# The first loads of a fused FFT-mix and gated MLP: a quarter on another queue, and two splits in another order

## The chip, the core and the metric

The kernel runs on one core of a Trainium2 chip. Such a core has a matrix engine (TensorE, PE in the profile, with its weight loads shown apart as PEld), VectorE (DVE), ScalarE (ACT), GpSimd (POOL) and SyncE (SP). Each engine works through its own list of instructions in order, and they wait for one another and for DMA transfers through semaphores. SyncE and GpSimd both issue DMA transfers here, each through a queue of its own, and all transfers share 16 DMA engines.

The metric is the device time of one launch in microseconds (us), the median over runs. The kernel before takes 355.21 us, the median of three runs between 354.94 and 356.22.

## The reference

For an input `x` of 2048 rows and 512 columns, the kernel computes a blend of two results, with a gate per row:

```python
x = A_x
g = _sigmoid((x * gate_w).sum(-1, keepdims=True))
# a: real part of a two-dimensional DFT of x
a_re, a_im = x @ dft_hid_re.T, x @ dft_hid_im.T
a = dft_seq_re @ a_re - dft_seq_im @ a_im
# b: gated MLP, 512 -> 1376 -> 512
b = (silu(x @ w1) * (x @ w3)) @ w2
return g * a + (1 - g) * b
```

All operands are float32.

## The kernel before, in words

**Precision.** TensorE multiplies float32 values that were rounded to a shorter form. To keep float32 accuracy, each operand is split into a rounded high part and a remainder. `high` (line 115) writes the high part with a copy on ACT; `low` (line 118) subtracts it from the source on DVE and writes the remainder; `split` does the one and then the other. A product of two operands is then three products on TensorE: high with high, high with remainder, remainder with high (line 129). The contraction of 256 rows takes two steps of 128, so a "chain" in this text is six products of 128x512 into one bank of PSUM.

**Stages.** The first and longest stage computes the two matrices `x @ w1` and `x @ w3` for 11 blocks of 128 columns, two halves of the rows each, with a scheme of seven products per two-by-two block (the factors of x are named B11, B12, B21, B22 and sums T1 to T4). Intermediate rows go out to HBM through GpSimd's queue and come back later. The second stage multiplies them by `w2` (H in the profile), the third does the DFT (O, E and Y), and the last one blends and writes the result.

**The opening.** This is where the change is made. The very first block is computed in another way than the rest, so that TensorE can begin on little data. The array `first` is laid out by the host as 3072 columns for 128 partitions: the first weight quarter (256 columns), B11 (1024), the fourth weight quarter (256), the second weight quarter (256), B21 (1024), the third weight quarter (256). SyncE loads it into `raw` in four loads of 768 columns (line 417). The first of them holds the first weight quarter and the first half of B11, the second one the second half of B11 and the fourth quarter. The third and fourth load do the same for B21. After them SyncE loads B12 and B22 (`xs_B`, line 174) and the next weights (`ws`, line 198).

While the loads are under way, TensorE runs nine products of a constant (line 423, `wps`, the number is `WARM`), whose result is not used, and ACT loads its table.

Then ACT and DVE split what has come, in a written order (the kernel sets the order of all instructions by hand). `high_by_both` has the first 256 columns of a half block rounded by ACT and the other 256 by DVE (line 465, CAST). `split_by_both` does this and then has DVE write the remainder of the whole half. Weights are split into `wa`, the fourth quarter into `a`, and x into `xo`. The chains (`C` in the profile) follow: the first with the first weight quarter and B11, the second with the fourth quarter and B11, the third with the second quarter and B21, the fourth with the third quarter and B21, and then the four chains with B12 and B22. In a chain's first step the first half of the block is used, in the second step the second half; the last of the six products needs the remainder of the second half.

The names and lines to follow: `raw<-first` (line 417) are the first loads, `wps` (423) the constant's products, line 115 ACT's rounding, 118 DVE's remainders, 465 DVE's share of rounding, 129 the products. Behind the edit the lines of the changed kernel are two lower.

Of the kernel before, what the change touches and what calls it, by code (L numbers as in the profile page):

```python
# [18 lines left out]
NTB = S // TB  # L19
NC = (F + P - 1) // P  # L20
NP2 = (NC + 1) // 2
WARM = 9
LOOK = 3
K = 9
TOL = 2.0 ** 40
# [5 lines left out]
def fnet_swiglu_gate_kernel(  # L31
# [27 lines left out]
    nc = tc.nc  # L59
# [26 lines left out]
    def bank(k, name):  # L86
        return psum.tile([P, 512], F32, tag=f"ps{k}", name=name)
# [26 lines left out]
    def high(hi, src):  # L114
        nc.scalar.activation(hi, src, AF.Copy)  # L115

    def low(hi, lo, src):
        nc.vector.tensor_sub(lo, src, hi.bitcast(F32))  # L118

    def split(hi, lo, src):  # L120
        high(hi, src)
        low(hi, lo, src)
# [20 lines left out]
    def flat(ap):  # L143
        return ap.rearrange("p a n -> p (a n)")
# [268 lines left out]
    ctx.enter_context(tc.manual_schedule())  # L413
    XO[0] = xo0.tile([P, 2, 7, 2, 512], F32R, tag="xo", name="xo0")
    raw = xo1.tile([P, 2, 6, 2, 512], F32, tag="xo", name="raw")[:, 0].rearrange("p i q n -> p (i q n)")
    for n in range(4):
        nc.sync.dma_start(raw[:, 768 * n : 768 * n + 768], first[:, 768 * n : 768 * n + 768])
    ST[0, "B11"], ST[0, "B21"] = raw[:, 256:1280], raw[:, 1792:2816]
    W0 = [raw[:, at : at + 256] for at in (0, 1536, 2816, 1280)]
    warm = nc.const_aps.tensor(1.0, [P, 512], mybir.dt.bfloat16)  # L420
    wps = bank(7, "wps")
    for n in range(WARM):
        nc.tensor.matmul(wps, warm[:, :P], warm, start=True, stop=True)
# [11 lines left out]
    def half(i, j, w, x, start):  # L435

        wp = lambda h, sl: a21[:, h, sl] if w is None else WA[0][:, h, w, sl]
        xp = lambda q, h: b12[:, h, q * 512 : (q + 1) * 512] if x is None else XO[0][:, h, x, q, :]  # L440
        hh, lh, hl = (0, 0), (1, 0), (0, 1)
        order = [(r, *p) for r in range(2)
                 for p in ((hh, lh, hl) if x is None or r and w == x else (hh, hl, lh))]
        for n, (r, u, v) in enumerate(order):
            matmul(C[i, j], wp(u, slice(r * P, (r + 1) * P)), xp(r, v),
                   start=start and n == 0, stop=not start and n == 5)

    def xo_half(k, q):
        i = OPS.index(k)
        return XO[0][:, 0, i, q], XO[0][:, 1, i, q], ST[0, k][:, q * 512 : (q + 1) * 512]  # L450
# [12 lines left out]
    def high_by_both(hi, lo, src):  # L463
        high(hi[:, :256], src[:, :256])
        nc.vector.tensor_copy(hi[:, 256:], src[:, 256:])

    def split_by_both(hi, lo, src):
        high_by_both(hi, lo, src)
        low(hi, lo, src)

    def w0_parts(w):
        return flat(WA[0][:, 0, w : w + 1]), flat(WA[0][:, 1, w : w + 1]), W0[w]

    high_by_both(*xo_half("B11", 0))
    high(*w0_parts(0)[::2])
    low(*xo_half("B11", 0))
    low(*w0_parts(0))
    split(*xo_half("B11", 1))
    half(0, 0, 0, 0, True)
    split(a21[:, 0], a21[:, 1], W0[3])  # L480
    half(1, 0, None, 0, True)
# [91 lines left out]
    n = NI - 1 - LOOK  # L573
# [1057 lines left out]
```

## Time and profile before

| | us |
|---|---|
| median of three runs | 355.21 |
| lowest, highest | 354.94, 356.22 |
| the profiled execution | 355.75 |
| its span, first to last instruction | 354.0 |
| PE busy in the span | 348.0 |
| DVE busy | 311.2 |
| ACT busy | 233.5 |
| first instruction on the constant, PE | 0.91 |
| first product of real data, PE | 5.17 |

The profile is of one execution. Times count from the start of the span, and the span is shorter than the device time, since the launch lies around it. A row of the timeline gives start, length, engine, line, operation, tile written and tiles read, shape and number, and in brackets the idle time of the engine ahead of it, with what ended that. A row of the busy time by stretch gives the stretch, its length, and then busy time and count for PE, PEld, DVE, ACT and POOL, the granted TensorE clock, the share of the DMA engines and GB/s. The ends of products are modelled: a product is shown 0.38 us long though in a full stream the next one starts earlier. The rows of DMA issues give the size of one and the time from its issue to its landing.

### The profile page before, as it was taken

The numbers are of one execution on the slowest core, as the hardware profiler recorded it, in microseconds if no ns is written. First come the engines' busy times: TensorE is split into PE (matmuls) and PEld (weight loads), VectorE is DVE, ScalarE is ACT, GpSimd is POOL, SyncE is SP. The second block draws the span as 40 slices with busy tenths as digits, with TensorE's granted clock in tenths as the row PEclk, the third lists the DMA queues.
The fourth block names the chain that finished last, engine by engine and source line by source line (L and its number), as shares of the span: only waits on it lengthen the run. The fifth ranks groups of instructions, "written<-read, shape, count | busy, mean of one in ns | idle before, by whom it ended". The sixth has DMA issues, their size and how long they took to land.

```text
span 354.0 us, 5152 instructions
## 1 busy us (share of the span) xinstructions
PE 348.0 (98%) x1718; PEld 303.7 (86%) x1718; DVE 311.2 (88%) x442; ACT 233.5 (66%) x395; POOL 73.3 (21%) x121
## 2 busy tenths in 40 slices
PE   8999999999999999999999999999999999999994
PEld 4888888888888888888888888888888888889994
DVE  4999989999869788888887899989969989998983
ACT  5875866556648687775433399642588988879940
POOL 0012333323111132111113763335011002000000
PEclk9999999999999999999999999999999999999999
DMA  7669865669645779999999149997649999999276
GB/s 279 254 244 357 319 261 212 224 240 332 222 120 192 250 218 390 408 400 402 373 382 291 58 126 373 410 365 241 237 120 362 416 411 406 411 409 348 100 262 219
DMA packets 33952, 103.03 MB, mean 291 GB/s; under 512 B 5874, under 2 KB 6276, under 8 KB 33924
## 3 DMA queue, kind: packets, MB, share of 16 engines
q1 hardware_dynamic: 26340, 75.91, 58.2%
q0 software_dynamic: 7584, 26.77, 20.6%
q8 instruction: 14, 0.23, 0.3%
q14 instruction: 14, 0.11, 0.1%
HBM read 78.02 MB, written 24.65 MB: 290 GB/s over the span
## 4 chain that ended last, share of the span: by engine, by line
PE 96%; DMA 1%; ACT 1%; DVE 0%; issue 0%; SPq 0%; ACTq 0%
PE H L129 32%; PE X L129 30%; PE Z L129 15%; PE Y L129 8%; PE Y L1304 4%; PE C L129 3%; PE O L129 3%; PE E L129 1%; DMA raw<-first 1%; PE Yodd L1304 0%; DVE h L408 0%; ACT w2t L115 0%; ACT u L369 0%; DVE r L1358 0%; ACT xo L115 0%
## 5 line engine op out<-in xcount | busy, mean ns | idle before, releaser
L129 PE MATMUL H<-w2t,ht 128*128 128x512 f32 (+1 forms) x528 | 114.1, 379 | 0.0
L129 PEld LDWEIGHTS H<-w2t,ht 128*128 128x128 f32 (+1 forms) x528 | 99.8, 189 | 14.2
L129 PE MATMUL X<-xo,wb 128*128 128x512 f32 x378 | 88.6, 379 | 0.0
L129 PEld LDWEIGHTS X<-xo,wb 128*128 128x128 f32 x378 | 71.4, 189 | 10.2
L765 ACT ACTIVATE t<-t 128x1024 f32<-128x1024 f32 (+1 forms) x68 | 67.3, 992 | 1.5 <-DVE t L754 1.4
L320 POOL DMA_DIRECT2D hs<-h x36 | 19.6, 545 | 88.7 <-DVE h L391 63.5
L404 ACT ACTIVATE h<-X 128x512 f32<-128x512 f32 x21 | 12.5, 596 | 32.2 <-PE X L129 21.8
L129 PE MATMUL Z<-xo,wa 128*128 128x512 f32 x126 | 30.7, 380 | 0.0
L129 PE MATMUL X<-xo,wa 128*128 128x512 f32 x126 | 30.8, 380 | 0.0
L115 ACT ACTIVATE ht<-hr 128x1024 fp32r<-128x1024 f32 x19 | 20.0, 1053 | 16.3 <-PE H L129 10.6
L129 PE MATMUL Y<-xo,wa 128*128 128x512 f32 x126 | 30.6, 379 | 0.0
L129 PE MATMUL Z<-xo,wb 128*128 128x512 f32 x126 | 30.6, 379 | 0.0
L381 DVE TENSOR_TENSOR u<-u,X 128x512 f32<-128x512 f32 x21 | 14.4, 686 | 17.9 <-PE X L129 13.4
L129 PEld LDWEIGHTS Z<-xo,wa 128*128 128x128 f32 x126 | 23.7, 189 | 3.8 <-ACT u L369 0.4
L129 PEld LDWEIGHTS X<-xo,wa 128*128 128x128 f32 x126 | 23.7, 189 | 3.6 <-DVE wa L118 0.3
L129 PEld LDWEIGHTS Y<-xo,wa 128*128 128x128 f32 x126 | 23.8, 189 | 3.4
L129 PEld LDWEIGHTS Z<-xo,wb 128*128 128x128 f32 x126 | 23.8, 189 | 3.4
L754 DVE TENSOR_TENSOR t<-t,rep 128x1024 f32<-128x1024 f32 x21 | 24.7, 1220 | 0.6 <-DMA t<-wt 0.6
L118 DVE TENSOR_TENSOR ht<-hr,ht 128x1024 fp32r<-128x1024 f32 x19 | 23.1, 1217 | 0.0
L115 ACT ACTIVATE wa<-ws 128x768 fp32r<-128x768 f32 x19 | 15.9, 838 | 6.2 <-PE Z L129 5.9
L752 DVE TENSOR_TENSOR t<-t,rep 128x512 f32<-128x512 f32 x30 | 19.0, 684 | 0.0
L756 DVE TENSOR_TENSOR t<-t,rep 128x1024 f32<-128x1024 f32 x16 | 18.7, 1220 | 0.0
(210 smaller groups left out, 519.6 us busy)
## 6 DMA issues: line engine op xcount, KB each, us to landing
t<-wt SPq DMA_DIRECT2D x60, 512.0 KB, 9.3
hr<-hs SPq DMA_DIRECT2D x19, 512.0 KB, 8.8
hs<-h POOLq DMA_DIRECT2D x36, 256.0 KB, 4.4
wbsp<-wb POOLq DMA_DIRECT2D x16, 512.0 KB, 4.8
wb<-wbsp SPq DMA_DIRECT2D x16, 512.0 KB, 9.4
xr<-xw SPq DMA_DIRECT2D x8, 512.0 KB, 11.6
xs_B<-xt SPq DMA_DIRECT2D x6, 512.0 KB, 6.5
ws<-w POOLq DMA_DIRECT2D x6, 512.0 KB, 4.0
```

The costliest lines, as they stand in the source:

```text
L115: nc.scalar.activation(hi, src, AF.Copy)
L118: nc.vector.tensor_sub(lo, src, hi.bitcast(F32))
L129: nc.tensor.matmul(ps.rearrange("p (n a) -> p n a", a=2), u, turns(v)[:, some], **kw)
L320: nc.gpsimd.dma_start(hs[c][:, b * TB : (b + 1) * TB], h)
L381: nc.vector.tensor_add(u4, u4, x)
L404: nc.scalar.activation(g1, x, AF.Silu)
L752: f(*(v[:, 512 * a : 512 * a + 512] for v in (t, t, r)))
L754: nc.vector.tensor_sub(t, t, r)
L756: nc.vector.tensor_add(t, t, r)
L765: nc.scalar.activation(t[:, :n], t[:, :n], AF.Abs, accum_out=acc[:, i : i + 1])
L1304: nc.tensor.matmul(to, u[i], v[j], start=n == k == 0, stop=n == len(terms) - 1 and k == 2, skip_group_check=True)
```

## The change

The first 256 columns of `first`, the first weight quarter, are loaded through GpSimd's queue. SyncE's first load holds only the 512 columns of the first half of B11; its three others are as they were. The quarter is split first, on ACT and then on DVE, and only then the first half of B11. The second half of B11 is rounded by ACT and DVE together, where before ACT rounded it alone. The number of products of the constant goes from nine to eight.

```diff
-WARM = 9
+WARM = 8
...
-    for n in range(4):
-        nc.sync.dma_start(raw[:, 768 * n : 768 * n + 768], first[:, 768 * n : 768 * n + 768])
+    for n, (lo, hi) in enumerate(((0, 256), (256, 768), (768, 1536), (1536, 2304), (2304, 3072))):
+        (nc.sync if n else nc.gpsimd).dma_start(raw[:, lo:hi], first[:, lo:hi])
...
-    high_by_both(*xo_half("B11", 0))
-    high(*w0_parts(0)[::2])
-    low(*xo_half("B11", 0))
-    low(*w0_parts(0))
-    split(*xo_half("B11", 1))
+    split(*w0_parts(0))
+    split_by_both(*xo_half("B11", 0))
+    split_by_both(*xo_half("B11", 1))
     half(0, 0, 0, 0, True)
```

The first rows of DVE's list, from the first instruction on data (`wa` is the quarter, `xo` is B11, `a` the fourth quarter; in brackets what an instruction waits for: DMAHW is a load of SyncE by its number, DMASW one of GpSimd, Activation is ACT):

```order
+L118 TENSOR_TENSOR wa_135<-raw,wa_135 128x256 [waits DMASW0_49,Activation_49]
 L465 CAST xo_100<-raw 128x256 [waits DMAHW0_49]
 L118 TENSOR_TENSOR xo_100<-raw,xo_100 128x512 [waits DVE_49,Activation_49]
-L118 TENSOR_TENSOR wa_135<-raw,wa_135 128x256 [waits Activation_49]
-L118 TENSOR_TENSOR xo_100<-raw,xo_100 128x512 [waits DMAHW1_49,Activation_49]
+L465 CAST xo_100<-raw 128x256 [waits DMAHW1_49]
+L118 TENSOR_TENSOR xo_100<-raw,xo_100 128x512 [waits DVE_49,Activation_49]
 L118 TENSOR_TENSOR a_128<-raw,a_128 128x256 [waits Activation_49]
```

The quarter's remainder moved from third place to the first, ahead of everything on x, and a second CAST stands ahead of the second remainder of B11.

The same place in ACT's list:

```order
+L115 ACTIVATE wa_135<-raw 128x256 [waits DMASW0_49]
 L115 ACTIVATE xo_100<-raw 128x256 [waits DMAHW0_49]
-L115 ACTIVATE wa_135<-raw 128x256
-L115 ACTIVATE xo_100<-raw 128x512 [waits DMAHW1_49]
+L115 ACTIVATE xo_100<-raw 128x256 [waits DMAHW1_49]
 L115 ACTIVATE a_128<-raw 128x256
```

The quarter's rounding moved ahead of that of x and waits for GpSimd's load, and the rounding of the second half of B11 has 256 columns where it had 512.

## Prediction

> **What bounds the kernel now.** I read the page first, for the engine that is full and the chain that ended last.
>
> ```profile
> span 354.0 us, 5152 instructions
> PE 348.0 (98%) x1718; PEld 303.7 (86%) x1718; DVE 311.2 (88%) x442; ACT 233.5 (66%) x395; POOL 73.3 (21%) x121
> ...
> PE 96%; DMA 1%; ACT 1%; DVE 0%; issue 0%; SPq 0%; ACTq 0%
> ...
> L129 PE MATMUL H<-w2t,ht 128*128 128x512 f32 (+1 forms) x528 | 114.1, 379 | 0.0
> ```
>
> TensorE is busy for 98% of the span and makes up 96% of the chain. One product of 512 columns costs 114.1 / 528 = 0.216 us in a full stream. The 1% of DMA and the ACT before the first product are where the edit lies, so next I read the chain of waits in order of time, and the busy time by stretch.
>
> ```profile
> 0.84 3.54 DMA raw<-first
> 4.38 0.02 issue
> 4.40 0.42 ACT xo L115
> 4.82 0.32 ACT wa L115
> 5.17 11.21 PE C L129 x48
> ...
> 9.37:207.22 197.85, 197.80 (x916) 172.59 (x915) 174.86 (x276) 123.57 (x207) 50.23 (x96) 1.00 0.76 274
> ```
>
> The first load lands at 4.38, two ACT instructions follow, and the first real product starts at 5.17. Behind 9.37 the TensorE column (the first after the length) is as long as the stretch, to 0.05 us in 198, and the chain stays on TensorE after it. So whatever the opening gains or loses by 9.37 arrives at the end undiminished, and nothing else in the edit can matter. The third view is the timeline of VectorE and of the weight loads over that opening.
>
> ```profile
> 4.40 0.29 DVE L465 CAST xo<-raw 128x256 fp32r<-128x256 f32 x1 [4.40 <-DMA raw<-first]
> 4.85 0.69 DVE L118 TENSOR_TENSOR xo<-raw,xo 128x512 fp32r<-128x512 f32 x1 [0.15 <-ACT xo L115]
> 5.46 0.42 DVE L118 TENSOR_TENSOR wa<-raw,wa 128x256 fp32r<-128x256 f32 x1
> 6.01 0.69 DVE L118 TENSOR_TENSOR xo<-raw,xo 128x512 fp32r<-128x512 f32 x1
> 6.62 0.42 DVE L118 TENSOR_TENSOR a<-raw,a 128x256 fp32r<-128x256 f32 x1
> 6.95 0.29 DVE L465 CAST xo<-raw 128x256 fp32r<-128x256 f32 x1
> 7.35 0.69 DVE L118 TENSOR_TENSOR xo<-raw,xo 128x512 fp32r<-128x512 f32 x1
> 7.96 0.42 DVE L118 TENSOR_TENSOR wa<-raw,wa 128x256 fp32r<-128x256 f32 x1
> 8.29 0.29 DVE L465 CAST xo<-raw 128x256 fp32r<-128x256 f32 x1
> 8.68 0.69 DVE L118 TENSOR_TENSOR xo<-raw,xo 128x512 fp32r<-128x512 f32 x1
> ...
> 5.17 1.27 PEld L129 LDWEIGHTS C<-xo,wa 128*128 128x128 f32 x5 [1.15 <-ACT wa L115]
> 6.75 0.19 PEld L129 LDWEIGHTS C<-xo,wa 128*128 128x128 f32 x1 [0.31 <-DVE xo L118]
> ...
> 9.43 0.30 PEld L129 LDWEIGHTS C<-xo,wa 128*128 128x128 f32 x2 [0.22 <-DVE xo L118]
> ```
>
> This is the bound of the opening, and it is VectorE, not the load: from 6.01 to 8.68 + 0.69 = 9.37 it runs one instruction after another, and twice (6.75 and 9.43) the sixth product of a chain waits for the remainder that VectorE has just written. The start of the first product at 5.17 is not what counts; what counts is when VectorE ends its second B11 remainder (6.01 + 0.69 = **6.70**), since its whole row to 9.37 and then TensorE hang on it.
>
> **The change part by part.** On VectorE the quarter's remainder now comes first, and the second half of B11 is rounded half by VectorE: one more CAST of 0.29 ahead of the second remainder, with a pause behind it, as 8.29 + 0.29 = 8.58 to 8.68 shows (0.10). ACT loses what VectorE gets:
>
> ```profile
> 4.72 0.40 ACT L115 ACTIVATE wa<-raw 128x256 fp32r<-128x256 f32 x1
> 5.34 0.64 ACT L115 ACTIVATE xo<-raw 128x512 fp32r<-128x512 f32 x1 [0.22 <-DMA raw<-first]
> ...
> 6.57 0.42 ACT L115 ACTIVATE xo<-raw 128x256 fp32r<-128x256 f32 x1 [0.29 <-DMA raw<-first]
> ...
> 7.93 0.42 ACT L115 ACTIVATE xo<-raw 128x256 fp32r<-128x256 f32 x1 [0.63 <-DMA raw<-first]
> ```
>
> The 0.64 becomes one of 0.42, as at 4.40 in the chain above.
>
> Let W be the time at which the quarter lands, X that of SyncE's first load, and N that of its second. The end of the second B11 remainder is the latest of three sums.
>
> From W: 0.02 to ACT (4.38 to 4.40), 0.40 rounding the quarter, 0.03 to VectorE (4.40 + 0.42 = 4.82 to 4.85), 0.33 for the quarter's remainder until the next starts (6.62 to 6.95), 0.29 + 0.10 for the cast, 0.61 for the first remainder (6.01 to 6.62), 0.29 + 0.10 for the new cast, 0.69 for the second remainder: W + 2.86. Against 6.70 the shift is **W - 3.84**.
>
> From X: 0.02 + 0.42 + 0.03 to the first remainder, then 0.61 + 0.29 + 0.10 + 0.69: X + 2.16, a shift of X - 4.54. SyncE's first load is a third shorter, but the quarter shares the DMA engines with it, the same bytes in all; I leave X at 4.38, a shift of -0.16.
>
> From N: 0.02 + 0.42 + 0.03 + 0.69 = N + 1.16. N was 5.34 - 0.02 = 5.32, so the shift is -0.22: the most that can be gained with the data that come when they do. Behind it the cover holds: the loads of B21 were rounded by ACT from 6.57 and 7.93, and VectorE started its remainders at 7.35 and 8.68, both later than these roundings' ends (6.99 and 8.35) by more than 0.3.
>
> So all hangs on W. Its price is not in the trace, since GpSimd issues no DMA before 23 us; the nearest rows are these (DMA issues by window, sizes and us from issue to landing; then GpSimd's first issue, and all those of one line; then the busy time of the first stretches, with DMA share and GB/s last):
>
> ```profile
> hs<-h POOLq DMA_DIRECT2D x1, 256.0 KB, 2.6
> hs<-h POOLq DMA_DIRECT2D x1, 256.0 KB, 5.7
> ws<-w POOLq DMA_DIRECT2D x1, 384.0 KB, 3.2
> raw<-first SPq DMA_DIRECT2D x1, 384.0 KB, 3.5
> 23.02 0.74 POOL L248 DMA_DIRECT2D wbsp<-wb  x1 [22.59 <-DVE wb L118]
> L320 POOL DMA_DIRECT2D hs<-h x36: 539/545/572, 34.9 to 189.2; - x36
> 1.50:2.00 0.50, 0.50 (x3) 0.15 (x1) 0.00 (x0) 0.50 (x1) 0.00 (x0) 1.00 0.41 37
> 2.00:2.50 0.50, 0.50 (x2) 0.15 (x1) 0.00 (x0) 0.23 (x2) 0.00 (x0) 1.00 0.81 92
> ```
>
> The lower end is 2.6, a 256 KB store from GpSimd in a quiet stretch (115 us); the upper end 5.7, the same store among other transfers (35 us). The quarter is 128 KB. Nearest in kind is the quiet 384 KB load from GpSimd at 3.2; a third of the bytes takes something off, but two rows put more on: GpSimd's first issue took 0.74 where later ones take 0.545, and until 2.5 us the engines are 41 to 81% busy while they move 37 to 92 GB/s, which the quarter meets together with SyncE's load. I take 3.3. SyncE's first issue at 0.84 is my start for GpSimd's too, so W = 4.14 and the shift is 4.14 - 3.84 = **+0.30 us**. For the range the ends are W = 3.44, where X governs (-0.16), and W = 6.54 (+2.70).
>
> [...]
>
> The ninth warming product costs nothing and its removal brings nothing: these products end at 0.91 + 4.01 = 4.92, and the first real one, needing the first cast, cannot start before W + 1.07 + about 0.05 = 5.26. Had W been 3.6, the ninth would have been in the way by about 0.2, which VectorE's row would have hidden again.
>
> ```profile
> 0.91 4.01 PE L423 MATMUL wps<-const-bfloat16-1.0 128*128 128x512 bf16 x9 [0.91 <-PEq L1618]
> 3.44 0.15 PEld L423 LDWEIGHTS <-const-bfloat16-1.0 128*128 128x128 bf16 x1 [0.27 <-issue]
> 3.87 0.15 PEld L423 LDWEIGHTS <-const-bfloat16-1.0 128*128 128x128 bf16 x1 [0.28 <-issue]
> 5.17 0.65 PE L129 MATMUL C<-xo,wa 128*128 128x512 f32 x1 [0.25 <-ACT wa L115]
> ```
>
> Issuing the quarter occupies GpSimd for 0.5 to 0.75 us when it has nothing else to do until 23.02. SyncE still issues four loads, so no later load of its queue moves; GpSimd's later transfers take the next semaphore in turn, and what each waits for is as long ago as before.
>
> The sum: 354.0 + 0.30 = 354.3 for the span, and with the 355.75 - 354.0 = 1.75 around it 356.05 for the profiled execution. That one lies 0.54 over the median of the runs shown, so the forecast is 355.21 + 0.30 = **355.5 us**. About 0.5%, or 1.8 us, is what a measurement can tell from no change.
>
> **The rivals.**
>
> The quarter lands early, by 3.84 or before. Then X or N governs, and the shift is -0.16 to -0.22: 355.0. For it speaks the quiet 2.6; against it the two cold stretches.
>
> The quarter lands late. GpSimd's queue is the one whose landings spread most (2.6 to 5.7 for one size), and the quarter has become the first link: ACT and VectorE each have it ahead of x in order, so B11, which may lie there since 4.4, stands behind it, and TensorE behind both. The kernel is slower by 1.8 us from W = 5.62, a landing of 4.8; at 5.0 the time is 0.84 + 5.0 - 3.84 = +2.0, or 357.2. Against it: the 5.7 came among other transfers, and before 2.5 us there is only SyncE's first load beside it.
>
> The clock. The warming products start 3.87 - 3.44 = 0.43 apart, twice the 0.216 of the stream, and the first real product is 0.65 long where the page has 0.379, so TensorE reached its full rate only about 4.3 us after 0.91. With eight products they end at 4.49, and the idle time ahead of 5.26 is 0.77 in place of 0.25. Should this start the count anew, full rate comes at 5.26 + 4.3 = 9.56. VectorE paces TensorE until W + 2.86 = 7.0; from there to 9.56 it would do 2.56 / 0.43 = 6.0 products in place of 11.9, so 5.9 x 0.216 = 1.27 more: +1.57, or 356.8. Against it: the granted clock stands at 1.00 in every stretch above, and 0.25 of idle did no harm. [...]
>
> That VectorE gets the extra cast for nothing, because it idles anyway, is excluded by its row from 6.01 on.
>
> **How the numbers follow.** The likeliest, W between 3.84 and about 5.2, has 0.59: 355.2 to 356.6, with 355.5 at its centre. Early landing 0.25 at 355.0; the clock 0.09 at 356.8; late beyond 5.2 has 0.07, at 357.2. The range for 8 in 10 takes the first two, widened by the scatter of runs of one kernel (354.94 to 356.22), and stops short of the last two: 354.7 to 356.7. Only the late quarter, or the clock on top of a quarter later than forecast, reaches 1.8 us: slower 0.07. Faster by that much is out of reach of -0.22, and scatter alone leaves it 0.02; the same 0.91.
>
> **What would show it.** In the profile of the changed kernel the landing of the quarter is the idle time that ends at ACT's first rounding: 4.1 to 4.2 by this forecast. VectorE's order should read remainder of the quarter, cast, remainder, cast, remainder, the last of them ending at W + 2.86, near 7.0 where it was 6.70; its row should still be without a gap from there to the second B21 remainder, and a weight load should still wait for that one, at about 9.7 where it was 9.43. TensorE's first product should start later than 5.17, its first six take less time from first to last than before. A first rounding at 3.8 or sooner would make me wrong towards faster; products 0.65 long and 0.43 apart after 7 us would be the clock; and a shift at 9.4 that is not found again at 207 would break the claim that TensorE passes it on.

## The result: slower by 1.1%

The changed kernel takes 359.15 us (median of four runs, 358.66 to 359.91) and the kernel before 355.26 (354.94 to 356.22). The ratio is 1.0107, with a 95% interval of 1.0079 to 1.0134: 3.9 us more, where 0.3 more was forecast and a range up to 356.7 given.

The page of the changed kernel's profiled execution, which took 358.66 us:

```profile
span 356.9 us, 5154 instructions
PE 348.9 (98%) x1717; PEld 304.8 (85%) x1717; DVE 311.3 (87%) x443; ACT 233.2 (65%) x395; POOL 70.1 (20%) x122
...
PE 97%; DMA 1%; DVE 1%; issue 0%; ACT 0%; DVEq 0%; POOLq 0%
```

The span is 2.9 us longer, though PE, PEld, DVE and ACT are each busy for as long as before, to 1.1 us. The chain of waits of the changed kernel, in order of time (start, length, what), tells where the first part went:

```profile
0.62 0.66 issue
1.28 4.22 DMA raw<-first
5.50 0.02 issue
5.53 0.42 ACT wa L115
5.95 0.02 issue
5.97 0.43 DVE wa L118
6.40 0.21 DVE xo L465
...
6.71 0.70 DVE xo L118
7.41 0.04 issue
7.45 12.10 PE C L129 x47
```

The first link is now the quarter. GpSimd issued it at 1.28, after 0.66 us in which it waited for nothing that the profile shows; SyncE's first load still goes out at 0.84. It landed 4.22 later, at 5.50. SyncE's half block of x was there long before, as the DMA issues of both queues show:

```profile
raw<-first SPq DMA_DIRECT2D x1, 256.0 KB, 2.9
...
raw<-first POOLq DMA_DIRECT2D x1, 128.0 KB, 4.2
```

That is 0.84 + 2.9 = 3.7 for x and 5.5 for half as many bytes of weights. VectorE's row follows from it:

```profile
5.97 0.43 DVE L118 TENSOR_TENSOR wa<-raw,wa 128x256 fp32r<-128x256 f32 x1 [5.97 <-ACT wa L115]
6.31 0.29 DVE L465 CAST xo<-raw 128x256 fp32r<-128x256 f32 x1
6.71 0.69 DVE L118 TENSOR_TENSOR xo<-raw,xo 128x512 fp32r<-128x512 f32 x1
7.31 0.29 DVE L465 CAST xo<-raw 128x256 fp32r<-128x256 f32 x1
7.71 0.69 DVE L118 TENSOR_TENSOR xo<-raw,xo 128x512 fp32r<-128x512 f32 x1
...
10.38 0.69 DVE L118 TENSOR_TENSOR xo<-raw,xo 128x512 fp32r<-128x512 f32 x1
```

The second B11 remainder ends at 7.71 + 0.69 = 8.40, where it was 6.70, and the second B21 remainder at 11.07, where it was 9.37: 1.70 late in both places, with no gap between. But TensorE loses more than that. Its rows over the same time:

```profile
0.91 3.59 PE L423 MATMUL wps<-const-bfloat16-1.0 128*128 128x512 bf16 x8 [0.91 <-PEq L1616]
6.75 0.45 PE L129 MATMUL C<-xo,wa 128*128 128x512 f32 x1 [2.25 <-DVE xo L465]
7.45 2.21 PE L129 MATMUL C<-xo,wa 128*128 128x512 f32 x5 [0.25 <-DVE xo L118]
9.45 2.33 PE L129 MATMUL C<-xo,a 128*128 128x512 f32 x6
11.62 2.75 PE L129 MATMUL C<-xo,wa 128*128 128x512 f32 x12
```

It idled for 2.25 us before the first real product. The second chain, six products without a wait, took 11.62 - 9.45 = 2.17 us from its start to the next, where six at 0.216 are 1.30. The busy time by stretch has the granted clock (third from the right); the kernel before is shown first, then the changed one:

```profile
8.00:11.00 3.00, 3.00 (x15) 2.49 (x14) 2.77 (x7) 2.36 (x5) 0.00 (x0) 1.00 1.03 419
```

```profile
7.50:8.00 0.50, 0.50 (x2) 0.47 (x3) 0.40 (x2) 0.35 (x2) 0.00 (x0) 0.79 1.05 408
8.00:11.00 3.00, 3.00 (x8) 2.37 (x8) 2.79 (x8) 2.23 (x5) 0.00 (x0) 0.50 1.03 415
11.00:11.50 0.50, 0.50 (x3) 0.38 (x3) 0.50 (x3) 0.50 (x1) 0.00 (x0) 0.80 1.07 442
```

From 8 to 11 us TensorE was busy without a break at half its clock and did 8 products; the kernel before did 15 in the same three microseconds. So from here on VectorE's row no longer paces TensorE: behind 7.45 none of its products waits. The two outer rows of the changed kernel place the edges: 0.79 means 0.21 us at half clock in its half microsecond and 0.80 means 0.20, so the half rate held from 7.79 to 11.20, for 3.41 us.

The shift can be followed by two marks of the chain, the first chain with B12 (it reads `b` and `wa`) and the first row of the second stage. Both are shown for the kernel before and then for the changed one:

```profile
11.04 1.46 PE L129 MATMUL C<-b,wa 128*128 128x512 f32 x6
```

```profile
14.21 1.46 PE L129 MATMUL C<-b,wa 128*128 128x512 f32 x6
```

That is 3.17 later. The second stage:

```profile
207.22 17.91 PE H L129 x83
```

```profile
210.25 19.86 PE H L129 x92
```

3.03 later, so the opening's loss reached it almost whole. What the profile accounts for is thus 1.70 by the late quarter and, as the remainder, 3.17 - 1.70 = 1.47 by the clock; experiment 1 tests this division.

### The profile page after: what moved, and what is told of

Same layout as the page of the kernel before. It is cut to its first block, busy times and chain, and to the rows that moved or that the text cites. A ratio compares the mean times of both kernels' runs of the same rounds, so it can differ in the third digit from the quotient of the medians.

```text
span 356.9 us, 5154 instructions
## 1 busy us (share of the span) xinstructions
PE 348.9 (98%) x1717; PEld 304.8 (85%) x1717; DVE 311.3 (87%) x443; ACT 233.2 (65%) x395; POOL 70.1 (20%) x122
## 4 chain that ended last, share of the span: by engine, by line
PE 97%; DMA 1%; DVE 1%; issue 0%; ACT 0%; DVEq 0%; POOLq 0%
PE H L129 32%; PE X L129 31%; PE Z L129 15%; PE Y L129 8%; PE Y L1302 4%; PE C L129 3%; PE O L129 3%; PE E L129 1%; DMA raw<-first 1%; DVE xo L118 0%; PE Yodd L1302 0%; DVE r L1356 0%; DVE wa L118 0%; ACT wa L115 0%; DVE xo L465 0%
```

## The experiments

Each ran beside the kernel before on the same chip; its median there was 355.43 in the first set (experiments 1 to 4), 355.56 in the second (5, 6, 7 and 11), 355.72 in the third (8, 9 and 10) and 355.27 for experiment 12. Ratios are of the means of the runs, with the 95% interval in brackets, so a ratio need not be that of two medians.

**1. Filling the idle time.** The changed kernel with more products of the constant.

```diff
-WARM = 8
+WARM = 15
```

> The changed kernel with 15 products of the constant in place of 8, so that TensorE has hardly an idle stretch before the first real product at 6.75. Nothing else is altered. Theory 1 (the loss is the late quarter, about 1.7 us, and on top of it a clock that falls to half for 3.4 us because TensorE idles from 4.50 to 6.75, about 1.45 us): no product behind the first one is spaced 0.43, VectorE's second B11 remainder still ends near 8.4, and the time is 1.7 us over the kernel before, 357.0. Theory 2 (the late quarter alone, the half-rate stretch does not reach the end): no change against the changed kernel, 359.1.

Measured: 357.39, ratio 1.0058 (1.0039 to 1.0077), 1.96 over the kernel before. TensorE in the stretch, and around the first real product:

```profile
8.00:11.00 3.00, 3.00 (x15) 2.36 (x13) 2.79 (x8) 2.21 (x6) 0.00 (x0) 1.00 1.03 416
```

```profile
6.74 0.52 PE L129 MATMUL C<-xo,wa 128*128 128x512 f32 x1
7.45 1.48 PE L129 MATMUL C<-xo,wa 128*128 128x512 f32 x5 [0.18 <-DVE xo L118]
8.77 1.46 PE L129 MATMUL C<-xo,a 128*128 128x512 f32 x6
```

Fifteen products in the three microseconds, at full clock, with the quarter landing at 5.50 as in the changed kernel. The chain with B12 starts at 12.73, 1.69 later than before: the late quarter alone. About half of the loss (1.9 of 3.9) was the clock, and it goes away without touching a load.

**2. Making the idle time without the late quarter.** The kernel before with fewer products of the constant.

```diff
-WARM = 9
+WARM = 5
```

> The kernel before with 5 products of the constant in place of 9; loads and splits as before. The last of them ends near 3.25 and TensorE then idles 1.9 us until 5.17, nearly as long as in the changed kernel (2.25). Theory 1 (idle time ahead of the first real product costs a stretch of half rate): full rate is lost for 3.4 us, some 7 products by 0.21 us, +1.4 us or 356.7, with the quarter not late at all. Theory 2 (the late quarter alone): the kernel before, 355.3, and 0.216 between the products from 7 us on.

Measured: 356.79, ratio 1.0032 (1.0018 to 1.0045), 1.36 more, with all loads as before:

```profile
4.96 2.93 PE L129 MATMUL C<-xo,wa 128*128 128x512 f32 x6 [1.74 <-ACT wa L115]
7.68 2.77 PE L129 MATMUL C<-xo,a 128*128 128x512 f32 x6
...
8.00:10.50 2.50, 2.50 (x7) 1.96 (x7) 2.11 (x6) 1.88 (x4) 0.00 (x0) 1.00 1.01 405
```

Theory 1's price held by the median, but the way there differs from what it says, so the agreement is in part luck: the profiled execution was the slowest of the eight (357.52), and its chain with B12 starts at 13.15, 2.11 later than before. Products are 0.43 apart from the first one on, until 10.8: here TensorE had not reached the full rate before the idle time, and got to it that much later. The granted clock reads 1.00 in this stretch all the same, with 7 products in 2.5 us; the column does not show a half rate that holds from the start.

**3. The quarter on SyncE's queue.** The changed kernel with five loads by SyncE.

```diff
-        (nc.sync if n else nc.gpsimd).dma_start(raw[:, lo:hi], first[:, lo:hi])
+        nc.sync.dma_start(raw[:, lo:hi], first[:, lo:hi])
```

> The changed kernel with the quarter as the first of five loads on SyncE's queue and none on GpSimd's; split order and 8 products of the constant as changed. Theory 1: with SyncE issuing at 0.84 a load of 128 KB lands by 3.7 to 4.0, so the quarter no longer governs; the half block of x, issued 0.43 later, lands near 4.4 and the second B11 remainder ends near 6.6 to 6.8: 355.3, within 0.3 us of the kernel before. Theory 3 (the order of the splits with its extra cast on VectorE is what costs): the loss stays, at least 1 us over the kernel before.

Measured: 356.27, ratio 1.0021 (1.0007 to 1.0036), 0.84 more. The queue was most of the loss, but 0.84 is left where at most 0.3 was expected. ACT's rows show the landings:

```profile
2.96 0.42 ACT L115 ACTIVATE wa<-raw 128x256 fp32r<-128x256 f32 x1 [0.72 <-DMA raw<-first]
4.10 0.42 ACT L115 ACTIVATE xo<-raw 128x256 fp32r<-128x256 f32 x1 [0.72 <-DMA raw<-first]
5.22 0.42 ACT L115 ACTIVATE xo<-raw 128x256 fp32r<-128x256 f32 x1 [0.70 <-DMA raw<-first]
...
7.72 0.42 ACT L115 ACTIVATE xo<-raw 128x256 fp32r<-128x256 f32 x1 [1.77 <-DMA raw<-first]
```

The quarter came at 2.94 and the second B11 remainder ended at 6.36, as worked out, 0.34 ahead of the kernel before. Then the first half of B21 landed only at 7.70, where the kernel before had it at 6.55, and VectorE stood idle for 1.02 us. The cover that the prediction found behind the second remainder was gone. That the five loads made this landing late is not shown: with exactly the loads of before it came by 6.17 in the profile of experiment 5 and only at 7.45 in that of experiment 6.

**4. The late quarter with the old order.** The changed kernel with the five split instructions as before.

```diff
-    split(*w0_parts(0))
-    split_by_both(*xo_half("B11", 0))
-    split_by_both(*xo_half("B11", 1))
+    high_by_both(*xo_half("B11", 0))
+    high(*w0_parts(0)[::2])
+    low(*xo_half("B11", 0))
+    low(*w0_parts(0))
+    split(*xo_half("B11", 1))
```

> The changed kernel with the five split instructions in the order of before (x ahead of the quarter, the second half rounded by ACT alone), but the quarter still on GpSimd's queue and 8 products of the constant. The quarter lands at 5.5, x at 4.1. Theory 1: the first product starts at 5.97 and the second B11 remainder ends near 7.0 in place of 8.40, so the late quarter costs 0.3 us; the idle time from 4.5 to 5.97 is 1.5 us, and if that too costs a stretch of half rate, 1.4 us come on top: 355.6 or 357.0. Theory 4 (a late quarter costs its lateness in any order): 357.0 without any product spaced 0.43.

Measured: 357.78, ratio 1.0068 (1.0047 to 1.0089), 2.35 more. The quarter landed at 6.03 in the profiled execution, still later than in the changed kernel, and the rows of VectorE and of the stretches read:

```profile
3.68 0.29 DVE L465 CAST xo<-raw 128x256 fp32r<-128x256 f32 x1 [3.68 <-DMA raw<-first]
4.13 0.69 DVE L118 TENSOR_TENSOR xo<-raw,xo 128x512 fp32r<-128x512 f32 x1 [0.15 <-ACT xo L115]
6.50 0.43 DVE L118 TENSOR_TENSOR wa<-raw,wa 128x256 fp32r<-128x256 f32 x1 [1.68 <-ACT wa L115]
7.02 0.69 DVE L118 TENSOR_TENSOR xo<-raw,xo 128x512 fp32r<-128x512 f32 x1
...
8.00:11.00 3.00, 3.00 (x8) 2.37 (x9) 2.79 (x8) 2.30 (x5) 0.00 (x0) 0.50 1.03 421
```

The second remainder ends at 7.71, 1.01 late, so with x ahead a quarter landing half a microsecond later cost 0.7 less than the change's order did. The half-clock stretch is there too, behind 2.05 us of idle. The time is above both figures of the expectation (355.6 and 357.0), which had taken the quarter at 5.5 and the remainder near 7.0.

**5. The eighth and ninth product.** The kernel before with `WARM = 8`, the third part of the change alone.

> The kernel before with 8 products of the constant in place of 9, nothing else. They end near 4.5 and TensorE idles about 0.7 us until 5.17 in place of 0.25. Theory 1 (what costs the clock is an idle time of one and a half to two us, as with 5 products): no product behind 6 us is spaced 0.43, 355.4, no difference to the kernel before. Theory 5 (the ninth product itself is what brings TensorE to full rate in time): part of the loss of the kernel with 5 products appears, +0.5 to +1.4, 356.0 to 356.8.

Measured: 355.39 against 355.56, ratio 1.0002 (0.9988 to 1.0016). The ninth product is worth nothing at an idle time of 0.53.

**6. The order alone.** The kernel before with the change's order of splits, four loads and nine products as before (the diff of experiment 4, read backwards).

> The kernel before with the order of the splits of the change alone (quarter first, the second half of B11 rounded by both engines); four loads by SyncE and 9 products as before. The quarter lands with the first load at about 4.38. Theory 1: the second B11 remainder ends at 4.38 + 2.86 = 7.24 in place of 6.70, the first product starts at 5.5, and the time is 0.5 us more, 355.9 to 356.0. Theory 6 (the order costs nothing, all of the loss is the queue and the clock): 355.4.

Measured: 355.62 against 355.56, ratio 1.0011 (0.9998 to 1.0024). In the profile the quarter was there at 4.16 and the second remainder ended at 7.05, that is 2.89 later, as the sum of the prediction has it (2.86); the chain with B12 began at 11.61, 0.57 later than in the profile of before. Of this the median shows 0.06, and the interval reaches to 0.85, so 0.5 lies inside it: the order costs little, and this run cannot say how little.

**7. A small load ahead of the quarter.**

```diff
+    dummy = const.tile([P, 8], F32, tag="dummy", name="dummy")
+    nc.gpsimd.dma_start(dummy, first[:, :8])
```

> The changed kernel with one more load on GpSimd's queue ahead of the quarter: 8 columns of the same array (4 KB) into a tile that nothing reads. The extra load is issued at 1.28 and the quarter behind it, at about 2.05. Theory 7 (the first transfer of GpSimd's queue pays for a first use, whoever it is): the small one lands 3 us or more after its issue, and the quarter 2.5 to 3.0 us after its own, near 4.8, earlier than in the changed kernel. Theory 8 (the quarter waits for SyncE's traffic on the DMA engines): the quarter again takes 4.2 us or more from its issue and lands after 6.2. The time itself is one look: 358 to 360 by either.

A single run: 360.19. The issues on GpSimd's queue:

```profile
raw<-first POOLq DMA_DIRECT2D x1, 128.0 KB, 5.9
dummy<-first POOLq DMA_DIRECT2D x1, 4.0 KB, 4.1
```

4 KB took 4.1 us, 128 KB in the changed kernel 4.2, so it is not the bytes. The quarter behind it, issued at 2.02, landed at 7.9. Theory 7's second half is refuted, since the second transfer fared worse than the first; what theory 8 says of the quarter holds, though it does not say why 4 KB should take so long.

**8. GpSimd's queue with the DMA engines to itself.** The changed kernel with SyncE's loads held back.

```diff
+    pad = const.tile([P, 8], F32, tag="pad", name="pad")
+    padd = dram.tile([P, 8], F32, tag="padd", name="padd")
+    ones = nc.const_aps.tensor(1.0, [P, 512], mybir.dt.bfloat16)
+    pads = bank(1, "pads")
+    for _ in range(8):
+        nc.scalar.activation(pads, ones, AF.Copy)
+    nc.scalar.activation(pad, ones[:, :8], AF.Copy)
+    nc.sync.dma_start(padd, pad)
```

> The changed kernel with SyncE's loads held back until about 7 us: a store of 4 KB, which waits for nine instructions of ACT on a constant, stands ahead of them on SyncE's queue. So the quarter on GpSimd's queue, issued at 1.28, has the DMA engines for itself. Only its landing is read; everything behind it is late by the delay, some 5 us. Theory 7 (the first transfer of GpSimd's queue pays for a first use): it again takes about 4 us from issue to landing. Theory 8 (it waits behind SyncE's traffic on the DMA engines): it takes 2.3 to 2.9 us and lands by 4.2.

The quarter's issue, and the busy time by stretch with DMA share and GB/s at the right:

```profile
raw<-first POOLq DMA_DIRECT2D x1, 128.0 KB, 2.4
...
2.00:3.00 1.00, 1.00 (x3) 0.30 (x2) 0.00 (x0) 0.96 (x3) 0.03 (x1) 1.00 0.25 61
3.00:4.00 1.00, 1.00 (x4) 0.30 (x2) 0.00 (x0) 0.94 (x3) 0.00 (x0) 1.00 0.18 70
4.00:5.00 1.00, 0.10 (x1) 0.00 (x0) 0.00 (x0) 0.97 (x2) 0.00 (x0) 1.00 0.00 0
```

Issued at the same 1.28, as the first transfer of its queue, on engines as unused as ever, it took 2.4 us. This settles it between the two: SyncE's loads are what made it 4.2. In the changed kernel the first packet of GpSimd's queue moved at 3.9, 2.6 us after its issue; here it moved at 2.7. So most of the delay came before the first packet. How the engines share out their time between the queues was not tried.

**9. The old order, the late quarter, and no idle time.** The kernel before with the split loads of the change and `WARM = 15`.

> The kernel before with two edits: the quarter on GpSimd's queue (SyncE's first load holds the half block of x alone), and 15 products of the constant in place of 9. Order of the splits as before. Theory 1: what was lost with this order and 8 products (2.35 us) falls apart into the quarter, landing at 5.5 to 6.0, which by the two rows of that run put the second B11 remainder 0.5 to 1.0 us later, and the clock with the rest; with the idle time filled only the first stays: 355.9 to 356.5, and no product spaced 0.43 behind 7 us. Rival (the lateness costs more than VectorE's row shows): 357.5 or more.

Measured: 356.12, ratio 1.0016 (1.0002 to 1.0030), 0.40 more. With the quarter on GpSimd's queue, landing at 5.75 in the profile, this kernel is within 0.2% of the one before. Against experiment 4, 1.95 of its 2.35 are gone. Not all of that is the clock: the quarter landed 0.28 earlier here, and the second remainder ended at 7.43 in place of 7.71, which leaves about 1.7 for the clock. Against experiment 1 the order decides how dear the lateness is, 0.4 or 2.0.

**10. Eleven products.** The changed kernel with `WARM = 11`.

> The changed kernel with 11 products of the constant in place of 8: they end near 5.8 and TensorE idles about 0.9 us before the first real product at 6.75, where the changed kernel has 2.25 and the one with 15 products next to nothing. Theory 1 (an idle time under about one us does not cost the rate): as with 15 products, 2.0 us over the kernel before, 357.5. Rival (only an unbroken row of products keeps the rate): half rate for 3.4 us again, 359.1.

Measured: a median of 359.45, but between 356.81 and 361.93 over four runs, ratio 1.0117 (1.0046 to 1.0188). The expectation missed. The quarter landed at 5.98 in the profile, the idle time was 1.45 rather than 0.9, and the rate fell, later than in the changed kernel:

```profile
7.23 0.45 PE L129 MATMUL C<-xo,wa 128*128 128x512 f32 x1 [1.45 <-DVE xo L465]
...
8.00:9.00 1.00, 1.00 (x5) 0.68 (x5) 0.90 (x3) 0.59 (x3) 0.00 (x0) 1.00 1.00 410
9.50:12.50 3.00, 3.00 (x8) 2.36 (x8) 2.88 (x7) 1.70 (x3) 0.00 (x0) 0.50 1.03 422
```

TensorE had been busy again for two microseconds when the half rate began, and it held while TensorE was fully busy. So the idle time is paid for afterwards, and by an amount that differs between runs: in order of time, 356.81, 358.66, 360.24 and 361.93, the four have mean granted clocks of 0.997, 0.995, 0.993 and 0.989.

**11 and 12. Two tries at a better kernel.** The quarter on ACT's queue with nine products (`nc.scalar` in place of `nc.gpsimd`), and the kernel before with eleven.

> The changed kernel with the quarter loaded by ACT's queue, issued ahead of the table load, and 9 products of the constant; split order and SyncE's four loads as changed. Theory 1: the quarter lands 2.1 to 2.9 us after 0.72, so by 3.6; x lands at 3.7 to 4.1, the second load at 5.2, and the second B11 remainder ends at 5.2 + 1.16 = 6.36, 0.34 ahead of the kernel before: 355.1, unless the third load lands late as it did with five loads on SyncE's queue (7.70), in which case 356.2. Theory 9 (any load on a second queue delays what SyncE loads): 356 or more.

> The kernel before with 11 products of the constant in place of 9, nothing else, as a try at a better kernel: they reach to 5.6, past the 5.17 at which the first real product could start, but the sixth product waits for VectorE until 6.75 anyway, and five products of 0.216 fit in between. Theory 1 (VectorE's row is the bound of the opening): no loss from the later first product, 355.6 in a session whose kernel before takes 355.6; and if some runs of the kernel before lose part of the full rate to their 0.25 us of idle, a little less, down to 355.2. Rival (the start of the first real product sets the end): 0.4 more, 356.0.

Measured: 355.95 against 355.56 (1.0008, 0.9999 to 1.0017) for the first, in which the quarter landed at 3.2, the second remainder ended at 6.27, and the first half of B21 came at 7.25. And 355.50 against 355.27 (1.0007, 0.9994 to 1.0020) for the second. Neither beats the kernel before. The first lies between its two expected times, 355.1 and 356.2, with the first half of B21 late again. The second does not decide between its theory and its rival: in its profile the constant's products were out of the way in time, and the first real one started at 4.96, 0.05 after ACT had rounded the quarter (4.91), as in the kernel before.

## Why the prediction was wrong

**What bounds the opening: right at full clock only.** In experiment 1 VectorE's row and the chain with B12 moved by the same 1.7, as the prediction has it. In the changed kernel itself TensorE at half clock became the bound: the weight load that was to wait for the second B21 remainder no longer waited. What the opening lost by the chain with B12 was still there at the second stage (3.17 and 3.03), so the claim that TensorE passes it on was right.

**The formula for the shift of VectorE's row: right.** W - 3.84 with the measured W of 5.50 gives 1.66, and 1.70 was measured. In experiment 6 the same sum, 2.86, was 2.89.

**W itself: wrong, and this is the step that failed first.** It was put together as 0.84 + 3.3 = 4.14. Both terms were too small: GpSimd issues its first transfer at 1.28, not at SyncE's 0.84 (0.44), and the landing was 4.22, not 3.3 (0.92). Together 1.36 of the missing time. The 3.3 leaned on a quiet load of 384 KB, and the argument against the late rival was that before 2.5 us there is only SyncE's first load beside the quarter. SyncE issues its four loads between 0.84 and 2.65, and experiment 8 shows that they are what counts: 2.4 without them, 4.1 to 4.7 with them, for 4 KB and 128 KB alike. The row of 5.7, among other transfers, was the nearer one in kind, though 4.2 is nearer to 3.2 in size. Nor is GpSimd's queue the one whose landings spread most, as the late rival has it: in the profile of before, SyncE's 512 KB loads `t<-wt` took 4.2 by the median between 100 and 120 us and 13.4 between 120 and 140. X, put at 4.38, came at 3.7; it did not govern.

**The rivals were priced apart, and they came together.** The late quarter stood at 0.07 and the clock at 0.09, each with a time of its own. The one causes the other: every microsecond that the quarter is late is a microsecond in which TensorE has nothing to do. At the W that was measured the idle time is 2.25 and not 0.77, and the clock's price of 1.27 (1.47 measured) comes on top of the quarter's 1.66. With both, 355.3 + 1.66 + 1.27 = 358.2, the forecast would have been 0.9 from the result in place of 3.6. The forecast's own list said "the clock on top of a quarter later than forecast" and gave it no chance of its own.

**The mechanism of the clock was half right.** The sign named for it, products 0.43 apart behind 7 us, is what the rows show. The count does not begin anew with the first product. In the profile of the changed kernel the full rate is there at first (the first product is 0.45 long, where the slow one of before was 0.65), is lost about one microsecond after work resumed, and returns 3.41 us later. That the price of 1.27 comes near 1.47 is in part luck, since it was worked out for 2.56 us of half rate in another place. The argument that the granted clock stood at 1.00 in every stretch before could not count either: it reads 1.00 there while the constant's products are 0.43 apart.

The stretches of experiments 4 and 10 have the same length, 3.42, worked out as above from the clock at their edges (0.73 in 7.50:8.00 and 0.85 in 11.00:11.50; 0.76 in 9.00:9.50 and 0.82 in 12.50:13.00). What the rows show beyond that: the constant's products start at 0.91 in experiments 6 and 9 as in the kernel before, and their spacing falls from 0.43 to 0.22 near 3.8 in experiment 6 (its nine took 3.51 us, against 4.01 before), near 4.9 in experiment 9 (4 products from 4.00 to 5.00, 6 from 5.00 to 6.00) and near 6.5 in experiment 1. So the full rate does not come a fixed time after the first of them. The half rate came after 2.25 us of idle in the changed kernel, 2.05 in experiment 4 and 1.45 in experiment 10. In experiment 6 the full rate was there before 0.98 us of idle and stayed: the second chain took 8.72 - 7.43 = 1.29 from its start to the next. No run lies between 0.98 and 1.45, and none shows what sets the 3.4 us or the moment at which the half rate begins.

**The ninth product** makes no difference that can be measured in the kernel before (experiment 5); the changed kernel with nine was not run. With the late quarter, fifteen products, up to the first real one at 6.74, kept the rate, and eleven, with 1.45 of idle behind them, did not.

**What is not accounted for.** The profile has 3.0 to 3.2 of the 3.9. The two profiled executions lie 2.9 apart, since that of the kernel before is 0.49 over its median (355.75 against 355.26) and that of the changed kernel 0.49 under its own (358.66 against 359.15); so the rest is scatter between executions. The other runs of the changed kernel have spans of 357.1 to 358.1 against this one's 356.9, and the quarter landed between 5.50 and 6.03 in the five profiles with these loads and nothing held back or put ahead. Nor did all four lose their clock in the same way. A stretch of 3.41 us at half takes 0.005 off the mean granted clock of such a span (1.71 of 356.9). Two of the four runs have 0.994 and 0.993; the other two have 0.999 and 1.000, which leaves no room for one, and yet took 359.91 and 358.87. A half rate that held from the start until behind the idle time, as in experiment 2, would leave no mark in this mean, but no trace of those two was kept.

## What to carry to other kernels

A transfer that starts a chain belongs on the queue whose issue comes first and whose landing has been seen to be steady under the traffic of that moment; what a transfer takes alone says little about it (128 KB: 2.4 us in experiment 8, 4.2 to 4.7 beside SyncE's loads). An idle time of TensorE near the start is to be priced twice, once for the wait and once for the slow stretch that can follow it (here 2.25 us of idle, then 3.41 at half clock), and a rival that causes another is to be added to it, not set beside it. Where a load may come late, work on data that are already there goes ahead of it in the order: with the idle time filled, a quarter landing at 5.5 to 5.75 cost 0.4 in the old order and 2.0 in the new one.

## What the runs showed that was not expected

GpSimd's first transfer is issued at 1.28 in every profile in which it loads something in the opening, 0.44 after the 0.84 of SyncE's first where nothing holds that back.

On GpSimd's queue, beside SyncE's loads, 4 KB took 4.1 us and 128 KB between 4.2 and 4.7; the second transfer of that queue, issued 0.74 after the first, took 5.9. Alone, 128 KB took 2.4. The first packet of that queue moved at 3.9 in the changed kernel, beside SyncE's loads, and at 2.7 in experiment 8, without them.

TensorE's half-rate stretch began after work had resumed, one microsecond in the changed kernel and about two in experiment 10.

The first half of B21, the third or fourth load in order, landed at 6.55 in the profile of before, but at 7.70 with five loads on SyncE's queue, at 7.25 with one on ACT's, and at 7.45 in experiment 6, where SyncE's loads are exactly those of before; in experiment 5, with those loads too, it was there by 6.17. Why it wanders by more than a microsecond is open; in experiment 3 it took back all that the early quarter had gained, and more.
